# Moving the first batch's early folds from GpSimd to VectorE, and the first weights ahead, in a fused attention, Fourier and MLP kernel

## The chip, the cores and the metric

The kernel runs on one core of a Trainium2 chip. The metric is the time of one execution on the device in microseconds (us), the median over several runs. Smaller is better. The engines are PE (TensorE, matmuls), DVE (VectorE), ACT (ScalarE), POOL (GpSimd) and SP (SyncE, which here only issues DMAs).

## The reference: what is computed

Chunked attention with a few memory keys, whose result goes through a Fourier mix over sequence and features, a normalisation, and a two-layer MLP with a residual:

```
# q, k, v: [4, 8, 768, 64]; mem_k, mem_v: [4, 8, 8, 64]
for each chunk of 32 queries:            # keys: 8 memory + 16 left + 32 own + 8 right
    a = softmax(q_c @ k_full.T / 8);  out_c = a @ v_full
x  = out as [4, 768, 512]
u  = x + real(fft(fft(x, axis=1), axis=2))
un = (u - mean) / sqrt(var + 1e-6)       # over the 512 features
result = u + relu(un @ w_ch1) @ w_ch2    # [512, 2048], [2048, 512]
```

## The kernel before

**Stages.** A batch b has 768 rows and 8 heads, taken as four pairs of heads. Pair n = 4b + i goes through `attention(n)`; after four pairs the batch goes through a Fourier stage (`first_fourier` for b = 0, `fourier(b)` for the others), then `columns_of`, and later `mlp(b)`.

*Attention.* Queries and keys are loaded by GpSimd's DMA queue (`e_load_qk`, L343 and L347, three buffers each), values by SP's (`e_load_v`, four buffers `va`). For batches 0 to 2 PE turns queries and keys by transposes (`turn`, L374: `trq`, `trk`), and ACT or DVE copies them out (`e_qT` L392, `e_kT` L417). For the last batch (TURNED = 3) SP turns them by a DMA transpose (`e_flip_q` L379, `e_flip_k` L383 into `kU`), and DVE copies the keys into place (`e_kT`, L412). For each half g of a pair: scores (`e_scores`, L430, into `sc`, of which there is one PSUM slot), exponentials on ACT (`e_exp`, L438), values (`e_values`, L454, into `xa` or, in the first batch's second halves, `xo`), and the normalisation on DVE (`e_norm`: reciprocal L464, product L465 into `xsb`). Half g holds row tiles 3g to 3g+2 of the batch.

*Fourier stage of the first batch.* The transform over rows and columns uses symmetry: columns are folded first. For each row half g and each parity `par` there is `g_zy` (L594: sum or difference of two column blocks), then for each `ab` a first fold `g_ff(..., last=0)` (L608 to L613: `zy` plus or minus reversed columns of `xsb`; it needs pairs 0 to 2) and a last fold `g_ff(..., last=1)` (L613 with `ff` as input; it needs pair 3 also). ACT casts the result to fp16 (`g_hi`, L629), DVE subtracts to get the rest (`g_lo`, L633, into `lo` or `hl`), and PE multiplies both with sine and cosine tables (`g_rows`, L666, into `ps`). GpSimd does a small extra row (`g_mid`, L639 to L642), which PE multiplies in `g_row` (L653). ACT and DVE evict `ps` (`e_up` L538, `e_rest` L543), then come the columns on PE (`e_columns`, L677, into `pm`), sums and statistics on DVE (L683, L691), the centred rows on ACT (L697).

*Later batches.* `fourier(b)` folds over rows as well; the mirrored half of the rows goes through HBM (`x_rows`, `x_back`, `xr`) and is added on the way back (L584).

*MLP.* PE computes `ph` (`e_ch1`, L739, in groups of 4 matmuls), ACT the relu (L747), PE `pc` (`e_ch2`, L754), DVE the residual (L779). The weights come in eight loads of 512 KB on GpSimd's queue (`w1` L975, `w2` L979), converted to fp16 on the way.

**What sets the order.** Nothing is issued in the order of the source. Every piece of work is a task of the class `Plan`: an engine, an expected cost, the tasks it comes after, the buffers it takes and gives back, and a rank. `Plan.order` plays the tasks against a clock made of these costs and lists them by planned start; they are emitted in that order. On the chip every engine then works through its own list strictly in order, and waits only where data or buffers demand it. Three arguments matter here: `behind=t` holds a task in the planning until task t has been placed; it makes no wait on the chip. `lag=x` makes the planner place a task only when what it comes after is x us old in planned time. A `filler` task (MLP matmuls) and the `idle` matmuls (L830, on zeros, keep PE going in the beginning, until the first `g_lo` is placed) fill PE where nothing else can be placed.

**What the change touches.** In `first_fourier` the early tasks of the first row half (g = 0) are on DVE and those of the second (g = 1) on GpSimd. In `weights` the loads of w1 are placed behind the keys of pair 5. `t_gate` is a tiny GpSimd copy that waits for the values of pair 3, so that loads for batch 1 don't start sooner.

Of the kernel before, what the change touches and what calls it, by code (L numbers as in the profile page):

```python
# [14 lines left out]
ALU = mybir.AluOpType  # L15
# [21 lines left out]
class Plan:  # L37
# [15 lines left out]
    def add(self, engine, cost, emit, after=(), take=(), give=(), rank=None, moved=0.0,  # L53
            loose=False, late=0.0, filler=False, behind=None, lag=0.0, pick=None, grain=0.1, head=1.0):
        t = dict(engine=engine, cost=cost, emit=emit, after=[a for a in after if a is not None],
                 take=take, give=give, rank=len(self.tasks) if rank is None else rank,
                 moved=moved, done=None, at=None, no=len(self.tasks), loose=loose,
                 late=late, filler=filler, behind=behind, lag=lag, pick=pick, grain=grain, head=head)
        self.tasks.append(t)
        return t  # L60
# [117 lines left out]
def kernel(  # L178
# [11 lines left out]
    nc = tc.nc  # L190
# [3 lines left out]
    P = 128  # L194
    NST = S // P
    NDT = DM // P
# [393 lines left out]
    def g_zy(par, g):  # L590
        if g == 0:
            zy_of[0, par] = fpool.tile([P, NST, P], FP32, tag="unT", bufs=2, name="zy0")
        xb, sl, eng = xs[0], slice(3 * g, 3 * g + 3), nc.gpsimd if g == 1 else nc.vector
        eng.tensor_tensor(zy_of[0, par][:, sl], xb[:, sl, 0:P], xb[:, sl, HD:HD + P],  # L594
                                ALU.add if par == 0 else ALU.subtract)

    def g_ff(par, ab, g, last):
        if (ab, g, last) == (0, 0, 0):
            ff_of[0, par] = fpool.tile([P, 2, NST, P], FP32, tag="fold", bufs=2, name="ff0")
        xb, sl = xs[0][:, 3 * g:3 * g + 3], slice(3 * g, 3 * g + 3)  # L600
        zy, ff = zy_of[0, par][:, sl], ff_of[0, par][:, ab, sl]
        eng = nc.gpsimd if g == 1 and not last else nc.vector
        plus = ab == par
        if last:
            plus = plus == (par == 0)
        if not last:
            if ab == 0:
                eng.tensor_copy(ff[:, :, 0], zy[:, :, 0])  # L608
            elif par == 0:
                eng.memset(ff[:, :, 0:1], 0.0)  # L610
        elif (par, ab) == (1, 1):
            eng.tensor_tensor(ff[:, :, 0], xb[:, :, P], xb[:, :, HD + P], ALU.subtract)
        eng.tensor_tensor(ff[:, :, 1:P], (ff if last else zy)[:, :, 1:P],  # L613
                                rev_ap(xb, 2 * P - 1 + HD * last, P - 1, [[DM, 3]]),
                                ALU.add if plus else ALU.subtract)

# [252 lines left out]
    def attention(n):  # L869
        nonlocal t_gate  # L870
        b, pr = seq[n]
        first = b == 0
        lq, lk = [add("POOL", 1.6 if b >= TURNED else 0.9, lambda i=i: e_load_qk(n, i),
                      take=(("qs", "ks")[i],), moved=3.1 if b >= TURNED else 1.2, grain=0.032 if b >= TURNED else 0.1, late=LATE if b else 2.0,
                      behind=t_gate if n == HP else t_xr[b - 2] if n == TURNED * HP else t_ck.get(n - 1),
                      rank={0: -4 + i, 1: -1.2 + 0.1 * i, 2: 10 + 0.1 * i}.get(n)) for i in range(2)]
        lv = add("SP", 2.5, lambda: e_load_v(n), [t_ones[n] if n < NV else None],
                 behind=t_x2.get(b - 2),
                 take=("va",), moved=2.6, grain=0.031, head=0.4, late=(0.0, 4.0, LATE, LATE)[b])
        t_lv[n] = lv  # L880
        t_ck[n] = lk
        if n == HP - 1:
            def e_gate():
                nc.gpsimd.tensor_copy(gate[64:65], va[n % NV][64:65, 1, NT - 1, 0:1])

            t_gate = add("POOL", 0.1, e_gate, [lv])
        mk = t_mk[n] = add("DVE", 0.2, lambda: e_mkT(n), [t_mkT, t_kTz[n % NKT], t_mk.get(n - 1)],
                           take=("kTb",), behind=t_norm.get((HP - 1, 1)) if n in (HP, HP + 1) else None)
        if b >= TURNED:
            eq = add("SP", 1.2, lambda: e_flip_q(n), [lq], take=("qT",), give=("qs",),  # L890
                     late=5.0, loose=True, behind=t_flip[0])
            t_flip[0] = tk = add("SP", 1.2, lambda: e_flip_k(n), [lk, t_uz], take=("kU",),
                                 give=("ks",), late=5.0, loose=True, behind=eq)
            ek = add("DVE", 0.6, lambda: e_kT(n), [tk, mk], give=("kU",))
        else:
            tq = add("PE", 0.40, lambda: e_turn_q(n), [lq, t_idb], take=("tr",), give=("qs",))
            dve = ("DVE", nc.vector.tensor_copy) if n < HP else ("ACT", None)
            eq = add("ACT", 0.80, lambda: e_qT(n), [tq], take=("qT",), give=("tr",),
                     rank=SINES - 0.5 if n == 0 else None)
            ktag = "acc" if first else "tr"  # L900
            tk = add("PE", 0.43, lambda: e_turn_k(n), [lk, t_idb, t_kz if n == 0 else t_kzs],
                     take=(ktag,), give=("ks",))
            ek = add(dve[0], 1.25 if dve[1] else 1.04, lambda: e_kT(n, dve[1]), [tk, mk],
                     give=(ktag,))
        for g in range(2):
            s_ = add("PE", 0.32, lambda g=g: e_scores(n, g), [eq, ek], take=("sc",),
                     give=("qT", "kTb") if g == 1 else ())
            t_sc[n, g] = s_
            t_exp[n, g] = x_ = add("ACT", 1.12, lambda g=g: e_exp(n, g),
                     [s_, t_masks, t_after.get(n)], take=("e1",), give=("sc",))  # L910
            tag = "mlp" if first and g == 1 else "xa"
            v_ = add("PE", 0.85, lambda g=g: e_values(n, g), [x_, lv, t_low[n % NV]], take=(tag,),
                     rank=len(plan.tasks) + (50 if (n, g) == (2, 1) else 25) if first else None,
                     give=("e1", "va") if g == 1 else ("e1",))
            take = ("xsb",) if g == 0 and n % HP == 0 else ()
            t_norm[n, g] = add("DVE", 0.78, lambda g=g: e_norm(n, g),
                               [v_, t_norm[n - n % HP, 0] if (n % HP, g) != (0, 0) else None],
                               take=take,
                               give=(tag,))
        return x_  # L920
# [47 lines left out]


    w2v = moe_w_ch2.rearrange("(ht p) m -> p ht m", p=P)  # L970
    t_w1, t_w2 = [], []

    def weights(n):
        if n == HP + 1:
            t_w1.extend(add("POOL", 0.7, lambda dt=dt: nc.gpsimd.dma_start(  # L975
                w1_sb[:, dt, :], moe_w_ch1[ts(dt, P), :]), moved=2.4, grain=0.32, late=2.0,
                behind=t_ck[n], rank=t_ck[n]["rank"] + 0.1) for dt in range(NDT))
        else:
            t_w2.extend(add("POOL", 0.7, lambda g=g: nc.gpsimd.dma_start(  # L979
                w2_sb[:, ts(g, 4), :], w2v[:, ts(g, 4), :]), moved=2.6, late=2.0,  # L980
                behind=t_ck[n], rank=t_ck[n]["rank"] + 0.1) for g in range(4))

    def first_fourier():
        t_rest, t_mid, t_row, pre = {}, {}, {}, {}
        for g in range(2):
            for par in range(2):
                early = ("DVE", "POOL")[g]
                zy = add(early, (0.5, 1.1)[g], lambda par=par, g=g: g_zy(par, g),
                         [t_norm[0, g], t_norm[1, g], t_sines],
                         take=("unT",) if g == 0 else (), rank=20.1 if g else None)  # L990
                for ab in range(2):
                    pre[par, ab, g] = add(early, (0.62 if ab == 0 else 0.5) + 0.8 * g,
                                          lambda par=par, ab=ab, g=g: g_ff(par, ab, g, 0),
                                          [zy, t_norm[2, g]], rank=20.2 + 0.1 * par if g else None,
                                          take=("fold",) if (ab, g) == (0, 0) else (),
                                          give=("unT",) if (ab, g) == (1, 1) else ())
            t_mid[g] = add("POOL", 0.9, lambda g=g: g_mid(g), [t_norm[2, g], t_norm[3, g]],
# [3 lines left out]
            for par in range(2):  # L1001
                for ab in range(2):
                    end = (ab, g) == (1, 1)
                    ff = add("DVE", 0.5 + 0.1 * par * ab,
                             lambda par=par, ab=ab, g=g: g_ff(par, ab, g, 1),
                             [pre[par, ab, g], t_norm[3, g]])
                    hi = add("ACT", 0.5, lambda par=par, ab=ab, g=g: g_hi(par, ab, g), [ff],
                             take=(("hl",), ("hT",))[par] if (ab, g) == (0, 0) else ())
                    lo = add("DVE", 0.48, lambda par=par, ab=ab, g=g: g_lo(par, ab, g), [hi],
# [206 lines left out]
```

The softmax here doesn't subtract the row's maximum and nothing guards it: scores larger than these inputs give would overflow.

## Time and profile before

The time is 289.14 us (median of 3 runs, 289.12 to 289.34). The profiled execution has a span of 287.7 us, at a PE clock of 1.00 throughout.

| engine | busy us | share of the span |
|---|---|---|
| PE | 272.2 | 95% |
| DVE | 169.5 | 59% |
| ACT | 159.9 | 56% |
| POOL | 65.7 | 23% |

The busy share of an engine is an average over stages that differ, so it has to be read by stage. Of PE's time, 8.2 us are the 35 `idle` matmuls, all before 34 us. The largest groups of work on PE are `ph` (88.5 us), `pc` (84.2 us, both with modelled ends), and `xa` (26.4 us). DMA moves 39.92 MB, at a mean of 139 GB/s, and at about 200 GB/s between 44 and 80 us.

A line of a timeline reads: start (us), duration (us), engine, line, operation, output <- inputs, shapes, count, and in brackets the idle time of the engine before it and what ended it. If several instructions are merged (x2), the duration is that of the whole stretch.

### The profile page before, as it was taken

Reading aid. Unit: us, or ns where it says so; the run is one execution under the profiler, and the core shown is the slowest. Engines: PE = TensorE matmul, PEld = TensorE weight load, DVE = VectorE, ACT = ScalarE, POOL = GpSimd, SP = SyncE. Lnnn points to the kernel's source line nnn. Section 1 sums busy time; section 2 is a strip of 40 time slices with the busy share of each in tenths; the row PEclk is TensorE's granted clock in tenths of the full one; section 3 lists DMA queues with packets and bytes.
Section 4 is the critical chain, followed back from the end, with each engine's and each line's share of the span. In section 5 each row is a group of like instructions: output and inputs, shape, how many; then the busy total and the mean of one; then the engine's idle time right before and its main releaser. Section 6 shows DMA issues by size and latency. Waiting matters only on the chain.

```text
span 287.7 us, 7165 instructions
## 1 busy us (share of the span) xinstructions
PE 272.2 (95%) x2947; PEld 172.2 (60%) x2947; DVE 169.5 (59%) x350; ACT 159.9 (56%) x286; POOL 65.7 (23%) x115
## 2 busy tenths in 40 slices
PE   0599889999999999999999999999999999999995
PEld 0476578865565777556766556566654644645644
DVE  7968999862159967958874984985672012012012
ACT  6887345788766676835764485517660721722710
POOL 8844794341210182261001020010020000000000
PEclk9999999999999999999999999999999999999999
DMA  6999999999998999999993756766142504003204
GB/s 108 198 184 162 180 154 204 203 201 196 207 189 219 171 199 153 164 112 238 173 209 86 166 113 108 175 107 195 21 85 84 106 0 117 32 34 100 51 36 109
DMA packets 116112, 39.92 MB, mean 139 GB/s; under 512 B 104560, under 2 KB 111472, under 8 KB 116080
## 3 DMA queue, kind: packets, MB, share of 16 engines
q1 hardware_dynamic: 93888, 23.54, 46.4%
q0 software_dynamic: 21472, 15.21, 32.9%
q10 hardware_dynamic: 720, 0.72, 0.8%
q8 instruction: 23, 0.38, 0.6%
q14 instruction: 9, 0.07, 0.1%
HBM read 37.36 MB, written 13.37 MB: 176 GB/s over the span
## 4 chain that ended last, share of the span: by engine, by line
PE 83%; DMA 6%; DVE 5%; POOL 4%; issue 1%; POOLq 0%
PE pc L754 28%; PE ph L739 26%; PE xa L454 7%; DMA qs<-in_q_dram 6%; PE ps L526 5%; PE pm L677 4%; PE sc L430 3%; DVE ff L613 2%; PE ps L666 2%; PE trk L374 2%; PE trq L374 1%; PE pc L760 1%; PE idle L830 1%; DVE hl L633 1%; DVE xsb L465 1%
## 5 line engine op out<-in xcount | busy, mean ns | idle before, releaser
L747 ACT ACTIVATE hT<-ph 128x384 f16<-128x384 f32 x128 | 62.0, 491 | 50.8 <-PE ph L739 49.9
L739 PE MATMUL ph<-unT,w_sb 128*128 128x384 f16 x512 | 88.5, 326 | 0.0
L754 PE MATMUL pc<-w_sb,hT 128*128 128x512 f16 x368 | 84.2, 380 | 0.0
L739 PEld LDWEIGHTS <-w_sb 128*128 128x128 f16 x512 | 48.4, 98 | 31.7 <-issue 0.6
L754 PEld LDWEIGHTS <-hT 128*128 128x128 f16 x368 | 34.5, 98 | 39.1 <-issue 0.2
L779 DVE SCALAR_TENSOR_TENSOR osb<-pc,rstd,xsb 128x512 f32<-128x512 f32 x23 | 17.2, 750 | 63.8 <-PE pc L754 61.6
L438 ACT ACTIVATE e<-sc,mbias 128x384 f32<-128x384 f32 x64 | 33.6, 577 | 22.7 <-PE sc L430 22.6
L454 PEld LDWEIGHTS xa<-va,e 128*64 128x64 f32 x672 | 22.5, 141 | 7.0 <-issue 5.6
L454 PE MATMUL xa<-va,e 128*64 128x65 f32 x672 | 26.4, 229 | 0.0
L697 ACT ACTIVATE un<-xsb,mu_s 128x512 f16<-128x512 f32 x24 | 17.2, 719 | 7.7 <-DVE mu_s L692 7.7
L538 ACT CAST up<-ps 128x386 f16<-128x386 f32 x16 | 9.6, 602 | 19.6 <-PE ps L526 17.4
L691 DVE BATCH_NORM_STATS2 st<-xsb 128x6 f32<-128x512 f32 x24 | 16.6, 692 | 0.8
L465 DVE TENSOR_TENSOR xsb<-xa,zs 128x384 f32<-128x384 f32 x28 | 15.6, 558 | 1.0
L464 DVE RECIPROCAL zs<-xa 128x6 f32<-128x6 f32 x28 | 5.3, 189 | 17.6 <-PE xa L454 17.6
L543 DVE TENSOR_TENSOR up<-ps,up 128x386 f16<-128x386 f32 x16 | 9.6, 598 | 9.2 <-ACT up L538 9.1
L683 DVE TENSOR_TENSOR xsb<-pm,xsb 128x512 f32<-128x512 f32 x15 | 10.0, 673 | 5.0 <-PE pm L677 5.0
L569 POOL DMA_DIRECT2D xr<-x_back x3 | 2.3, 780 | 46.6 <-DMA x_back<-x_rows 46.6
L430 PEld LDWEIGHTS <-kTb 64*128 64x128 bf16 x384 | 7.7, 97 | 8.7 <-issue 6.8
L430 PE MATMUL sc<-qT,kTb 64*128 64x64 bf16 x384 | 11.6, 196 | 0.9 <-POOL va L315 0.9
L516 DVE TENSOR_TENSOR lo<-ff,hi 128x768 f16<-128x768 f32 x12 | 11.4, 954 | 1.5 <-ACT hi L511 1.3
L486 DVE TENSOR_TENSOR zy<-xsb 128x768 f32<-128x768 f32 x12 | 11.4, 955 | 0.2
L503 DVE TENSOR_TENSOR ff<-pq 128x762 f32<-128x762 f32 x12 | 11.3, 947 | 0.0
(153 smaller groups left out, 355.1 us busy)
## 6 DMA issues: line engine op xcount, KB each, us to landing
va<-in_v_dram SPq DMA_DIRECT2D x32, 220.0 KB
w_sb<-in_moe_w_ch_dram POOLq DMA_DIRECT2D x8, 512.0 KB, 14.7
out_dram<-osb SPq DMA_DIRECT2D x12, 256.0 KB
qs<-in_q_dram POOLq DMA_DIRECT2D x12, 192.0 KB, 6.8
ks<-in_k_dram POOLq DMA_DIRECT2D x12, 192.0 KB, 6.7
x_rows<-xsb POOLq DMA_DIRECT2D x3, 768.0 KB, 5.5
xr<-x_back POOLq DMA_DIRECT2D x3, 768.0 KB, 5.4
out_rows<-osb SPq DMA_DIRECT2D x9, 256.0 KB
```

The lines of the kernel that those rows point to most:

```text
L430: nc.tensor.matmul(sc[:, hh, t6, :], kT[r0:r0 + 64, t, :], qT[r0:r0 + 64, ts(t, 64)], start=True, stop=True, tile_position=(r0, 0))
L438: nc.scalar.activation(e1[:, :, :, ts(half, 32)], sc[:, :, 0:6, ts(half, 32)], AFT.Exp, bias=mbias[:, half:half + 1], scale=1.0 / math.sqr ...
L454: nc.tensor.matmul(xa[64 * half:64 * half + 64, st, hh, 0:65], e1[:, hh, t6, :], v1[:, hh, 6 * g + t6, 0:65], start=True, stop=True)
L465: nc.vector.tensor_tensor(xs[b][:, 3 * g:3 * g + 3, 2 * pr * D:(2 * pr + 2) * D] .rearrange("p s (h d) -> p s h d", h=2), xa[:, :, :, 0:D] ...
L526: nc.tensor.matmul(out_[:, sp, :], part[:, ab, sp * 3 + st, c0:c1], tab[:, sp, st, :], start=(st == 0 and i == 0), stop=(st == 2 and i == 1))
L677: nc.tensor.matmul(pm[:, par, :], lhs, rhs[:, par, :], start=(im == 0), stop=(im == 3))
L691: nc.vector.bn_stats(st6, xs[b][:, kt, :])
L697: nc.scalar.activation(un, xs[b][:, kt, :], AFT.Identity, bias=mu_of[b][:, kt, 0:1], scale=-1.0)
L739: nc.tensor.matmul(ph[:, 0:384], w1_sb[:, dt, ts(ht, P)], unT_of[b][:, dt, sh * 384:(sh + 1) * 384], start=(dt == 0), stop=(dt == NDT - 1))
L747: nc.scalar.activation(hT_of[b, sh][:, ht, :], ph[:, 0:384], AFT.Relu, bias=0.0, scale=-1.0)
L754: nc.tensor.matmul(pc_of[b, sh, stl], hT_of[b, sh][:, ht, ts(stl, P)], w2_sb[:, ht, :], start=(ht == 0), stop=(ht == NHT - 1))
L779: nc.vector.scalar_tensor_tensor(osb, pc, rstd_of[b][:, st:st + 1], xs[b][:, st, :], ALU.mult, ALU.add)
```

## The change

The change has three parts.

1. The early folds of the second row half (g = 1), which are two `g_zy` and four `g_ff(..., last=0)` with their small copies and a memset, go from GpSimd to DVE. On GpSimd only `g_mid` remains of this stage. Their planned costs and ranks become those of the first half.
2. The loads of w1 are no longer placed behind the keys of pair 5, but behind the task `t_mark`, the first last-fold of the second row half (par 0, ab 0) on DVE; what follows the keys of pair 5 is now placed behind the last load of w1 (`t_ck[n] = t_w1[-1]`). It is meant to put the weights where GpSimd is done with this stage.
3. The copy of DMA-turned keys (`e_kT` of the last batch) gets `lag=4.0`: it is placed at least 4 us after the planned landing of the transpose, so that DVE should not stand in front of a transpose that is late.

```diff
     def g_zy(par, g):
         ...
-        xb, sl, eng = xs[0], slice(3 * g, 3 * g + 3), nc.gpsimd if g == 1 else nc.vector
-        eng.tensor_tensor(zy_of[0, par][:, sl], xb[:, sl, 0:P], xb[:, sl, HD:HD + P],
+        xb, sl = xs[0], slice(3 * g, 3 * g + 3)
+        nc.vector.tensor_tensor(zy_of[0, par][:, sl], xb[:, sl, 0:P], xb[:, sl, HD:HD + P],
                                 ALU.add if par == 0 else ALU.subtract)

     def g_ff(par, ab, g, last):
         ...
-        eng = nc.gpsimd if g == 1 and not last else nc.vector
         ...
-        eng.tensor_tensor(ff[:, :, 1:P], (ff if last else zy)[:, :, 1:P],
+        nc.vector.tensor_tensor(ff[:, :, 1:P], (ff if last else zy)[:, :, 1:P],
                                 rev_ap(xb, 2 * P - 1 + HD * last, P - 1, [[DM, 3]]),
                                 ALU.add if plus else ALU.subtract)
         ...
-            ek = add("DVE", 0.6, lambda: e_kT(n), [tk, mk], give=("kU",))
+            ek = add("DVE", 0.6, lambda: e_kT(n), [tk, mk], give=("kU",), lag=4.0)
         ...
-    t_w1, t_w2 = [], []
+    t_w1, t_w2, t_mark = [], [], []

     def weights(n):
         if n == HP + 1:
             t_w1.extend(add("POOL", 0.7, lambda dt=dt: nc.gpsimd.dma_start(
                 w1_sb[:, dt, :], moe_w_ch1[ts(dt, P), :]), moved=2.4, grain=0.32, late=2.0,
-                behind=t_ck[n], rank=t_ck[n]["rank"] + 0.1) for dt in range(NDT))
+                behind=t_mark[0], rank=t_ck[n]["rank"] + 0.1) for dt in range(NDT))
+            t_ck[n] = t_w1[-1]
         ...
-                early = ("DVE", "POOL")[g]
-                zy = add(early, (0.5, 1.1)[g], lambda par=par, g=g: g_zy(par, g),
+                zy = add("DVE", 0.5, lambda par=par, g=g: g_zy(par, g),
                          [t_norm[0, g], t_norm[1, g], t_sines],
-                         take=("unT",) if g == 0 else (), rank=20.1 if g else None)
+                         take=("unT",) if g == 0 else ())
                 for ab in range(2):
-                    pre[par, ab, g] = add(early, (0.62 if ab == 0 else 0.5) + 0.8 * g,
+                    pre[par, ab, g] = add("DVE", (0.62 if ab == 0 else 0.5),
                                           lambda par=par, ab=ab, g=g: g_ff(par, ab, g, 0),
-                                          [zy, t_norm[2, g]], rank=20.2 + 0.1 * par if g else None,
+                                          [zy, t_norm[2, g]],
         ...
+                    if (par, ab, g) == (0, 0, 1):
+                        t_mark.append(ff)
```

Beside the named instructions the change moves others, since the planner works the whole order out anew. Read from the instruction lists as built: PE has 28 `idle` matmuls instead of 35; a key turn and both scores of pair 4 stand ahead of the first batch's columns, where one key turn did; from pair 6 on attention and MLP matmuls are interleaved in another way; and in the last batch the scores of pairs 12 to 15 stand further back.

More of the change, by code (lines that the diff above doesn't have):

```diff
@@ L607, in g_ff @@
             if ab == 0:
-                eng.tensor_copy(ff[:, :, 0], zy[:, :, 0])
+                nc.vector.tensor_copy(ff[:, :, 0], zy[:, :, 0])
             elif par == 0:
-                eng.memset(ff[:, :, 0:1], 0.0)
+                nc.vector.memset(ff[:, :, 0:1], 0.0)
         elif (par, ab) == (1, 1):
-            eng.tensor_tensor(ff[:, :, 0], xb[:, :, P], xb[:, :, HD + P], ALU.subtract)
-        eng.tensor_tensor(ff[:, :, 1:P], (ff if last else zy)[:, :, 1:P],
+            nc.vector.tensor_tensor(ff[:, :, 0], xb[:, :, P], xb[:, :, HD + P], ALU.subtract)
+        nc.vector.tensor_tensor(ff[:, :, 1:P], (ff if last else zy)[:, :, 1:P],
                                 rev_ap(xb, 2 * P - 1 + HD * last, P - 1, [[DM, 3]]),
```

## The prediction

> **What bounds the kernel now.** I read the slices of the page first, then busy time by stage, then the timelines of VectorE (DVE), GpSimd (POOL) and TensorE (PE) between 22 and 56 us, then the chain of waits. The slices of PE, VectorE and GpSimd (7.2 us each):
>
> ```profile
> PE   0599889999999999999999999999999999999995
> DVE  7968999862159967958874984985672012012012
> POOL 8844794341210182261001020010020000000000
> ```
>
> PE is full from slice 7 to the end; before that it isn't. Busy time by stage (columns PE, PEld, DVE, ACT, POOL, then clock, DMA share, GB/s) says where the free time lies:
>
> ```profile
> 30.00:37.00 7.00, 5.68 (x76) 3.95 (x75) 6.90 (x15) 1.99 (x5) 5.07 (x12) 1.00 1.21 178
> 37.00:44.00 7.00, 6.17 (x70) 5.38 (x68) 7.00 (x14) 3.07 (x7) 7.00 (x10) 1.00 0.90 159
> 44.00:50.00 6.00, 5.97 (x82) 5.03 (x80) 5.49 (x13) 3.42 (x6) 2.39 (x4) 1.00 1.04 203
> 50.00:56.00 6.00, 6.00 (x106) 4.76 (x105) 5.68 (x13) 4.94 (x9) 1.39 (x2) 1.00 1.11 205
> ```
>
> From 47 to 284 us PE waits for nothing (every later stage reads 10.00 of 10.00, and no PE wait is listed after 45 us). So the end is the time at which PE is filled, plus a fixed amount of matmuls, plus a tail of 3 us. Only what PE wastes before 47 us can be gained. Between 30 and 44 us VectorE is the full engine: it folds the first batch. Its timeline there:
>
> ```profile
> 27.59 1.81 DVE L613 TENSOR_TENSOR ff<-zy,xsb 128x381 f32<-128x381 f32 x2
> 30.08 2.95 DVE L613 TENSOR_TENSOR ff<-zy,xsb 128x381 f32<-128x381 f32 x2
> 33.77 1.02 DVE L613 TENSOR_TENSOR ff<-ff,xsb 128x381 f32<-128x381 f32 x2
> 34.93 0.56 DVE L465 TENSOR_TENSOR xsb<-xo,zs 128x384 f32<-128x384 f32 x1
> 37.81 2.61 DVE L633 TENSOR_TENSOR hl<-ff,hl 128x384 f16<-128x384 f32 x2
> 42.76 1.01 DVE L633 TENSOR_TENSOR hl<-ff,hl 128x384 f16<-128x384 f32 x2
> ```
>
> and GpSimd's:
>
> ```profile
> 26.65 2.34 POOL L594 TENSOR_TENSOR zy<-xsb 128x384 f32<-128x384 f32 x2
> 31.64 0.98 POOL L613 TENSOR_TENSOR ff<-zy,xsb 128x381 f32<-128x381 f32 x1
> 37.44 2.58 POOL L613 TENSOR_TENSOR ff<-zy,xsb 128x381 f32<-128x381 f32 x2
> 39.96 0.68 POOL L347 DMA_DIRECT2D ks<-in_k_dram  x1
> 40.63 2.20 POOL L975 DMA_DIRECT2D w_sb<-in_moe_w_ch_dram  x4
> ```
>
> The same VectorE fold takes 1.02 us for two when GpSimd rests, and 1.81 to 2.95 when GpSimd runs a fold at the same time; the subtraction of L633 goes from 1.01 to 2.61. GpSimd's help is paid for on the engine it helps. One more pair, from the chain of waits:
>
> ```profile
> 53.66 17.74 DMA qs<-in_q_dram
> 71.44 0.53 PE trq L374 x16
> ```
>
> The queries of pair 7, issued behind all weights, land as PE comes to turn them, with about 0.1 us to spare. This is no loss now, but it is the next wall.
>
> **What the skill says.** "SBUF — State Buffer", section "Who interferes with whom": a VectorE instruction with two SBUF inputs takes its second one through a read interface that GpSimd shares, and the pair is locked for a whole instruction. Trace: agrees; folds and subtractions (two SBUF inputs) stretch, the normalisation L465 (one input in PSUM) stays at 0.56. "DMA: Bandwidth & Descriptors", section "Issuing engines are not separate DMA queues": all DMAs run on the same 16 engines and interleave. Trace: agrees, the mean DMA share is 0.9 to 1.2 from 22 to 80 us, so starting the weights sooner brings little new bandwidth.
>
> **Part 1: early folds to VectorE.** Spacing of starts is the price: 0.47 us a fold (36.88 to 37.81 for two), 0.48 for zy, 0.1 for the small copy, 0.05 for the memset. Added: 2 x 0.48 + 4 x 0.47 + 0.25 = 3.1 us. Removed, by form: the four ff<-zy mean 1.23 against 0.547 free (2.7 us), the four hl 0.945 against 0.547 (1.6), two small copies 0.48 against 0.16 (0.6): 4.9 us. Net 1.8 us less, and the new zy also use 0.6 us of idle before 26.20.
>
> Walked in the built order, with PE and ScalarE as in the trace: kTb copy from 24.34 to 25.5; two zy 26.5; normalisation (0.7) and fold 27.75; wait for the values (PE done 27.97), normalisation 28.8; two folds 29.9; normalisation 30.7; two folds 31.6; last normalisation 32.3 (now 35.4). Then 0.94 + 1.41 + 0.54 + 1.1 + 0.47 + 1.04 + 1.41: the second half's first subtraction can start at 39.2, those of its first three parts end at 39.7, 40.2, 40.65, and, after a fold, two kTb copies and one eviction, the last at 42.5.
>
> PE: the four first-half groups of 12 rows matmuls (1.02 us each) run from 35.5, after mid rows and a key turn that now stand in front of them, to 39.6; the second half 39.8 to 43.85, bound by VectorE at its start, then by PE. Next in PE's order come the scores of pair 4, a query turn (0.46), the second scores. There is one PSUM slot for scores, and ScalarE does two evictions (until 44.6) and the exponentials (1.0) before it is free: PE stands from 44.6 to 45.65 (new wait). Columns start at 45.95, now 47.23.
>
> Gain, counted as waste. From 31.36 (end of the last values) to the columns: now 15.87 us, of which useful 0.47 query turn + 0.3 + 2.4 mid rows + 8.12 rows (96 x 0.0845) + 0.47 key turn = 11.8, wasted 4.1 (nine fill matmuls 1.5, GpSimd's mid 1.3, VectorE 0.9, rest 0.4). Then: 14.6 us, with 1.02 more useful work in it (two scores, one query turn), wasted 1.8. **Gain 2.3 us.** PE is full from there, so it reaches the end one for one. Fifth and sixth columns need sums that VectorE gives at about 52.5: 0.3 us lost. PE's order has four fewer changes of kind (0.1 us each, as ph x4 takes 0.76 at a change and 0.65 inside a run): 0.3 to 0.4 won. Sum 2.3 us.
>
> **Part 2: weights behind the first fold.** The mark orders the planner only; no wait is added. In the built order the four loads stand right behind the mid operations, about 33.9 instead of 40.63, and the keys of pair 5 stand before everything (about 28 instead of 39.96). Queued behind are the queries of pair 6, w2, those of pair 7. PE first needs w1 at about 55.4; the slowest w1 landing was 13.3 us, so 49.5: nothing on the path. Pair 7's queries: PE asks for them at 71.44 - 2.3 - 0.65 = 68.5 (built order: two scores and one values more, three ph groups fewer ahead). The chain of loads starts 6.7 us sooner and without 192 KB of keys (1 us) in front, but shares the engines with one and a half v loads more (0.85 MB at 180 GB/s, 4.2 us, minus half a v load, 1.4): landing at about 66.5, bounds 64 (no sharing) and 70.5 (full engines give no gain but that of the missing keys). I take 66.5: cost nothing, hidden by ph.
>
> **Part 3: copies of turned keys later.** A planning delay of 4 us for four VectorE copies of 0.43 us. No VectorE wait for these transposes is in the trace, so nothing is removed. In the built order the last batch's values end some 20 matmuls (3 us) later; MLP matmuls stand in their place. Behind them are folds (PE has 8.6 us of work against a VectorE chain of 6.5) and mirrored rows, which landed at 196.8 for a first use at 206.9. Cost nothing.
>
> **The rivals.**
> (a) The stretch isn't GpSimd's doing: folds stay at 1.23 us, VectorE gets 3.1 us more, minus 0.6 of idle. PE fills 2.5 us later, minus 1.0 for work moved ahead: 290.6, slower. Against it: the same form at 0.547 as soon as GpSimd rests. Chance 0.06. With it go stalls later on that I can't see, as the copies in part 3 (290): 0.04.
> (b) Transfers are the next wall: pair 7 lands at 69 to 70.5, PE stands 0.5 to 2 us: 288.1. For it: DMA share near 1. Chance 0.2.
> (c) What I gain is lost again at score slot, bank and VectorE waits: within 0.2%. Chance 0.06.
> (d) The score wait doesn't come up, as ScalarE is earlier: 1 us more, 285.8. Chance 0.08.
>
> **The numbers.** Likeliest, at 0.56: 289.14 - 2.3 = 286.8 us. Range 285.5 to 288.8, which takes in most of (b) and (d) and leaves out (a) and part of (c). Faster by over 0.2% (under 288.56): 0.56 + 0.08 + 0.2 = 0.84; within 0.2% 0.06; slower 0.10.
>
> **What would show it.** Right: ff<-zy and hl at 0.55 us; last L465 of the first batch near 32.3; 28 fill matmuls for 35; w1 issued near 34; columns from about 46 with the scores of pair 4 before them; PE without a gap after 47. Wrong: folds still over 1 us; a PE gap in front of pair 7's query turn near 68 us, released by its DMA; VectorE waiting for a transposed key; a gap in front of the last batch's rows or MLP.

## The result and the profile after

The changed kernel takes **286.27 us** (median of 5 executions, 286.13 to 286.98) against 289.34 before (5 executions beside it, 289.12 to 290.34): a ratio of 0.9897, 95% interval 0.9874 to 0.9919. Run a second time, among the last experiments, it took 286.74 (286.09 to 287.19) against 289.13 before: 0.9915, 0.9898 to 0.9932. The prediction was 286.8, in a range of 285.5 to 288.8. Ratios are taken over executions within 1.5% of a kernel's fastest; some of the kernels below stand still in some executions and not in others, so I compare medians of all their executions.

The slices of the page for TensorE (PE) and GpSimd (POOL), 7.1 us each:

```profile
PE   0599998999999999999999999999999999999995
POOL 8844643131210183170001020101002000000000
```

Counted from 0, PE's slices 4 and 5 (29 to 43 us) were 8 and are 9, slice 6 has become 8, and GpSimd's 7 and 9 in slices 4 and 5 are 6 and 4. Busy time by stage, with the columns of the prediction (length, PE, PEld, DVE, ACT, POOL, clock, DMA share, GB/s):

```profile
30.00:37.00 7.00, 6.70 (x108) 5.56 (x107) 6.64 (x19) 2.54 (x5) 5.82 (x13) 1.00 1.20 208
37.00:44.00 7.00, 6.77 (x90) 6.34 (x89) 6.61 (x18) 4.65 (x9) 2.61 (x4) 1.00 1.08 212
44.00:50.00 6.00, 5.15 (x86) 4.45 (x85) 4.91 (x12) 3.68 (x8) 1.92 (x3) 1.00 1.14 197
50.00:56.00 6.00, 5.76 (x115) 4.55 (x112) 5.86 (x14) 4.13 (x7) 1.26 (x2) 1.00 1.23 197
```

PE was busy 11.85 us of the 14 from 30 to 44, and is now busy 13.47. In the next two stages it is idle for 0.85 and 0.24 us. The timeline of VectorE has the operations that were stretched before:

```profile
31.35 0.56 DVE L465 TENSOR_TENSOR xsb<-xo,zs 128x384 f32<-128x384 f32 x1
36.66 1.02 DVE L612 TENSOR_TENSOR ff<-zy,xsb 128x381 f32<-128x381 f32 x2
41.87 0.55 DVE L632 TENSOR_TENSOR hl<-ff,hl 128x384 f16<-128x384 f32 x1
```

Folds and subtractions are at 0.55 us (1.02 for two); none is longer. The last normalisation ends at 31.9 (35.5 before), the last subtraction at 42.4. On GpSimd's timeline nothing but the middle sums stands ahead of the weights, which go out at 33.10 instead of 40.63:

```profile
33.10 2.20 POOL L974 DMA_DIRECT2D w_sb<-in_moe_w_ch_dram  x4
```

And PE's timeline, with its only gaps after 45 us, and the query turn of pair 7, which before started 0.04 us after its data had landed (71.40 and 71.44):

```profile
45.32 0.35 PE L430 MATMUL sc<-qT,kTb 64*128 64x64 bf16 x12 [0.85 <-ACT e L438]
52.36 0.39 PE L676 MATMUL pm<-cosD,dn 128*128 128x256 f16 x2 [0.24 <-DVE xsb L682]
67.79 0.51 PE L374 MATMUL trq<-ident_b,qs 96*64 96x96 bf16 x16
```

The score slot's wait is there, as forecast (0.85 us), so is the fifth column's (0.24), and the query turn waits for nothing. The columns start at 45.60 (47.23 before).

One caution on that pair of traces. Twelve score matmuls take 0.50 us in the beginning and 0.35 later; the short durations set in at 17.9 us in the profiled run of after and at 19.1 in that of before, with the same order of work. (0.50 is also what they take at a granted clock of 0.50, in a timeline shown below; in the beginning the profile lists a granted clock of 1.00.) That moves the first batch's last value matmuls by 0.5 us and is not the change's doing: in the second profile of after they come 0.2 us later than before, and its columns at 45.85. So the two traces give the change 2.7 and 3.0 us.

A useful way to split every run below is at the first column matmul: what comes before it is the first batch's stage, and **the rest**, from there to the end of the span, is a fixed amount of work plus whatever PE waits for. The time is the median of a kernel, the other columns are of its one profiled execution, and they can differ: before, part 2 alone and part 3 alone have medians within 0.3 us of each other and columns at 47.23, 46.24 and 47.66. So I take a start of the columns to be good to about 0.7 us either way.

| kernel | time, us | columns start | rest | PE waits in the rest (0.2 us and more) |
|---|---|---|---|---|
| before | 289.34 | 47.23 | 240.5 | none |
| after | 286.27 | 45.60 | 239.0 | 0.24 |
| after, again | 286.74 | 45.85 | 239.0 | 0.23 |
| part 1 alone | 291.77 | 46.29 | 243.4 | values 2.43, turned keys 0.38 |
| part 2 alone | 289.42 | 46.24 | 240.4 | none (an execution of 288.30) |
| part 3 alone | 289.62 | 47.66 | 240.6 | 0.27 |
| parts 1 and 2 | 286.60 | 46.08 | 238.8 | 0.2 |
| before, GpSimd writes only | 287.09 | 45.06 | 240.3 | none |
| after, spare GpSimd folds | 290.48 | 49.80 | 239.0 | 0.3 |
| after, weights early | 290.54 | 46.35 | 239.2 | 0.24 (an execution of 287.23) |
| part 1, weights late | 293.28 | 46.13 | 245.3 | turned keys 3.99, queries 0.69 |
| parts 1 and 3 | 289.00 | 47.49 | 240.7 | values 1.70 |
| parts 1 and 3, weights late | 288.01 | 45.83 | 239.6 | 0.37 (an execution of 287.15) |
| after, scores later | 288.10 | 44.51 | 241.8 | sums of the second batch 1.57, 0.24 |

### The profile page after: what moved, and what is told of

It reads as the page before. It is cut to its first block, busy times and chain, and to the rows that moved or that the text cites. A ratio compares the mean times of both kernels' runs of the same rounds, so it can differ in the third digit from the quotient of the medians.

```text
span 284.6 us, 7154 instructions
## 1 busy us (share of the span) xinstructions
PE 269.5 (95%) x2940; PEld 171.6 (60%) x2940; DVE 166.2 (58%) x359; ACT 158.2 (56%) x286; POOL 57.5 (20%) x106
## 4 chain that ended last, share of the span: by engine, by line
PE 81%; DMA 7%; DVE 6%; SPq 2%; ACT 2%; issue 1%; POOL 0%; DVEq 0%; POOLq 0%
PE ph L738 30%; PE pc L753 29%; PE xa L454 7%; PE ps L526 5%; DMA va<-in_v_dram 4%; PE pm L676 4%; PE sc L430 2%; DMA qs<-in_q_dram 2%; DVE ff L612 1%; PE trq L374 1%; SPq L356 1%; PE trk L374 1%; DMA out_dram<-osb 1%; DVE xsb L682 1%; PE pm L577 1%
## 5 line engine op out<-in xcount | busy, mean ns | idle before, releaser
L738 PEld LDWEIGHTS <-w_sb 128*128 128x128 f16 x512 | 48.6, 98 | 32.3 <-issue 0.8
L690 DVE BATCH_NORM_STATS2 st<-xsb 128x6 f32<-128x512 f32 x24 | 16.6, 692 | 0.7
L511 ACT CAST hi<-ff 128x768 f16<-128x768 f32 x12 | 10.0, 831 | 4.3 <-DVE ff L503 4.3
```

What stands on the lines that cost most here:

```text
L690: nc.vector.bn_stats(st6, xs[b][:, kt, :])
L738: nc.tensor.matmul(ph[:, 0:384], w1_sb[:, dt, ts(ht, P)], unT_of[b][:, dt, sh * 384:(sh + 1) * 384], start=(dt == 0), stop=(dt == NDT - 1))
```

## The experiments

### The parts one by one

The theory was that part 1 carries the whole gain. Each part of the diff shown above was put on the kernel before by itself, and parts 1 and 2 together.

**Part 1 alone** (the folds on VectorE; w1 still behind `t_ck[n]`, no lag).

> Part 1 alone: early folds on VectorE, w1 placed behind the keys of pair 5 as before, no delay for the turned keys. In its order w1 is issued right behind those keys, about 28 us, ahead of the mid operations. Theory A (the gain is the end of the stretch of VectorE folds, carried one for one to PE): VectorE folds at 0.55 us, 286.3 to 287.0, so at least 2.3 of the 3 us. Rival B (the gain is that of the weights being placed better): 288.5 or more. Rival C (the planning delay of the copies is needed, without it VectorE stands before a transpose): 288 or more with a VectorE wait for kU.

Measured: 291.77 us (22 executions, 289.31 to 296.38), ratio 1.006 (1.0037 to 1.0084). That is slower than before. Yet the folds do what they should: they take 0.55 us, and the columns start at 46.29. All of the loss is in the rest, which is 4.6 us longer than with parts 1 and 2. Its PE waits:

```profile
PE xa L454 <- DMA va<-in_mem_v_dram: 2.4, 1, 2.4
PE sc L430 <- DVE kTb L412: 0.4, 1, 0.4
```

The first is new: values of pair 6, at 68.1 to 70.53 us. Around it, busy time by stage:

```profile
68.00:72.00 4.00, 1.57 (x33) 1.50 (x31) 0.08 (x1) 0.65 (x2) 0.00 (x0) 0.79 0.96 183
72.00:76.00 4.00, 4.00 (x75) 2.64 (x71) 1.19 (x4) 2.24 (x4) 0.63 (x1) 0.78 0.94 158
```

The third column from the right is PE's clock: 0.79 and 0.78. After the gap it was granted at half for about 3.4 us (in slices of 1 us it reads 0.66, 0.50, 0.50, 0.63), so 1.7 us more are lost. With 2.43 and 0.38 that makes 4.5 us, against the 4.6 that the rest is longer (parts 1 and 2 wait 0.24 us there, which this run does not).

Why are the values late? SyncE's own timeline, which issues them, in part 1 alone:

```profile
29.47 14.32 SPq L356 DMA_DIRECT2D va<-in_v_dram  x2
60.51 0.32 SPq L365 DMA_DIRECT2D va<-in_mem_v_dram  x1
```

and in the whole change:

```profile
30.83 3.94 SPq L356 DMA_DIRECT2D va<-in_v_dram  x2
51.31 0.31 SPq L365 DMA_DIRECT2D va<-in_mem_v_dram  x1
```

In part 1 alone the keys of pair 5 no longer wait behind GpSimd's folds, and w1, placed behind them, goes out at 28.78. The issue of a pair of value loads that starts right after it stands for 14.32 us, and the last piece of pair 6 is issued at 60.51 and arrives at 70.39 (9.88 us in the chain of waits), while PE wants it at 67.8. In the whole change it is issued at 51.31 for a use at 67.04. In the kernel before it was issued at 36.94 for a use at 76.50.

**Part 2 alone** (`behind=t_mark[0]` on the kernel before) and **part 3 alone** (`lag=4.0`).

> Part 2 alone: folds of the second half stay on GpSimd. The instruction order is nearly that of the kernel before, because the mark falls where GpSimd is busy with folds. Theory A: 289.1 to 289.4, no change. Rival B: 287.5 or less.

> Part 3 alone: the copies of turned keys placed 4 us later in the plan. No VectorE wait for these transposes is in the trace of before, so theory A: 289.0 to 289.6, no change beyond a few changes of kind on PE (0.1 us each; two pieces more in PE's order). Rival C: 288.5 or less.

Measured: 289.42 us (ratio 0.9994, 0.9977 to 1.001) and 289.62 (1.0007, 0.9989 to 1.0025). Neither moves the time. In part 2 alone w1 goes out at 39.64 instead of 40.63: GpSimd's folds still stand ahead of it, so the new place changes hardly anything.

**Parts 1 and 2** (the whole change without the lag).

> Parts 1 and 2, without part 3. Theory A: as the whole change, 286.0 to 286.6, and no VectorE wait for kU over 0.3 us. Rival C: 287 or more, with VectorE waiting for a transposed key and PE behind it.

Measured: 286.60 us (six executions, 285.91 to 290.70; ratio 0.9901, 0.9874 to 0.9929), as the whole change. So part 2, worth nothing alone, is needed beside part 1, and part 3 moves the median by nothing that can be measured. Two of the six executions stand apart, at 288.06 and 290.70, where none of the eleven of the whole change is above 287.19; six are too few to say whether the lag keeps such executions away.

### Is it GpSimd's reading that stretches VectorE?

**Before, with GpSimd writing only.** The six early folds of row half 2 become memsets, with every other engine's list as before. They are zeros then, and this half's part of the Fourier rows is left out:

```diff
+        if g == 1:
+            nc.gpsimd.memset(zy_of[0, par][:, sl], 0.0)
+            return
         ...
+        if g == 1 and not last:
+            nc.gpsimd.memset(ff, 0.0)
+            return
```

> The kernel before, with the six early folds of row half 2 on GpSimd replaced by GpSimd memsets of the same tiles, so that the even and odd folds of that half are zeros and its part of the first batch's Fourier rows is left out; TensorE, VectorE and ScalarE keep the order of before. Theory A (GpSimd's folds stretch VectorE's work on the same row half, and that holds the rows): the VectorE folds and low parts of row half 1 and 2 between 31 and 42 us fall from 1.0 to 1.5 us each to about 0.55 us, the columns start some 2 to 3 us earlier, and the time is 286.5 to 287.7 us. Rival (VectorE's work in that stretch is slow for another reason, or the rows are held by something else): the VectorE operations stay at 1.0 us and over, and the time stays at 289 to 290 us.

Measured: 287.09 us, ratio 0.9922 (0.9908 to 0.9937). GpSimd's timeline and VectorE's beside it:

```profile
28.77 0.79 POOL L607 MEMSET ff<- 128x384 f32 x2
34.48 0.77 POOL L607 MEMSET ff<- 128x384 f32 x2
```

```profile
29.43 1.01 DVE L619 TENSOR_TENSOR ff<-zy,xsb 128x381 f32<-128x381 f32 x2
34.48 1.01 DVE L619 TENSOR_TENSOR ff<-ff,xsb 128x381 f32<-128x381 f32 x2
35.41 1.01 DVE L639 TENSOR_TENSOR hl<-ff,hl 128x384 f16<-128x384 f32 x2
```

VectorE's folds and subtractions are at 0.55 us (1.01 for two), in the old order, even while GpSimd writes at that very moment. The columns start at 45.06, 2.2 us sooner, and the rest is that of before (240.3): a gain of 2.4 us with no new order at all. A rival would be that GpSimd, with less to do, is merely quicker with the middle sums, for which PE waited 1.29 us in before. But there GpSimd had itself waited 1.19 us for VectorE's normalisation before it could start them, so that wait too goes back to VectorE.

**After, with spare folds on GpSimd.** Their results go into a tile that nothing reads; the lists of the other engines are those of after.

```diff
+        if g == 1:
+            nc.gpsimd.tensor_tensor(spare, xb[:, sl, 0:P], xb[:, sl, HD:HD + P], ALU.add)
         ...
+        if g == 1 and not last:
+            nc.gpsimd.tensor_tensor(spare[:, :, 1:P], zy[:, :, 1:P],
+                                    rev_ap(xb, 2 * P - 1, P - 1, [[DM, 3]]), ALU.add)
```

> The kernel after, in which GpSimd repeats the six early folds of row half 2 into a spare tile that nothing reads; the order of TensorE, VectorE, ScalarE and SyncE is that of after, and the first weights are issued behind the spare folds, some 4 to 5 us later. Theory A (work of GpSimd on the rows stretches VectorE's): VectorE's folds of 0.55 us go back to 1.0 us and over while GpSimd folds, the columns start 1.5 to 2.5 us later than in after, and the time is 288 to 289.5 us. Rival (what helped was another order of the work, not the missing GpSimd folds): VectorE's folds stay at 0.55 us and the time is 286 to 287 us.

Measured: 290.48 us (289.86 to 291.75), ratio 1.0044 (1.0028 to 1.006). GpSimd and VectorE:

```profile
35.70 5.23 POOL L619 TENSOR_TENSOR spare<-zy,xsb 128x381 f32<-128x381 f32 x4
```

```profile
37.02 1.80 DVE L615 TENSOR_TENSOR ff<-zy,xsb 128x381 f32<-128x381 f32 x2
38.74 1.34 DVE L638 TENSOR_TENSOR hl<-ff,hl 128x384 f16<-128x384 f32 x1
40.01 0.95 DVE L610 COPY ff<-zy 128x3 f32<-128x3 f32 x1
```

The same operations, 1.02 for two and 0.55 in after, are stretched again, and even a copy of three columns goes from 0.16 to 0.95. The columns start at 49.80. The rest is 239.0, that of after: the 4.2 us that the first stage loses reach the end one for one. 0.6 of them arise in the first 14 us, before any spare fold runs. The loss is well over the 1.5 to 2.5 us I expected, and VectorE's list accounts for it: its first subtraction of the second row half starts at 43.20, against 38.99 in after, and 3.2 us of this delay arise between a small copy at 36.15 (35.11 in after) and that subtraction, beside the four spare folds. PE's wait of 1.70 us for ScalarE's half of a fold belongs to it, since ScalarE had waited for VectorE's fold. PE's waits for late middle sums (0.32 and 0.23) and for a query (0.71) come before these and add nothing, as PE then waits for VectorE all the same. The rival, that only the order helped, is out in both directions.

### What part 2 is for: the weights and the values

**After, with the weights early.** The four loads of w1 are issued inside the load of the keys of pair 5; the planner still counts them at their old place, so every other engine's list is that of after.

```diff
+        if (n, i) == W1_AT:                      # (HP + 1, 1)
+            for dt in range(NDT):
+                nc.gpsimd.dma_start(w1_sb[:, dt, :], moe_w_ch1[ts(dt, P), :])
         ...
-            t_w1.extend(add("POOL", 0.7, lambda dt=dt: nc.gpsimd.dma_start(
-                w1_sb[:, dt, :], moe_w_ch1[ts(dt, P), :]), moved=2.4, ...
+            t_w1.extend(add("POOL", 0.7, lambda dt=dt: None, moved=2.4, ...
```

> The kernel after with one thing moved: GpSimd issues the four first weight loads right behind the key load of pair 5 (about 28 us, as in part 1 alone) and not behind the middle sums (33.1 us). The order of TensorE, VectorE, ScalarE and SyncE is that of after. Theory V (in part 1 alone the early weights hold up the value loads: one SyncE issue of value rows was blocked for 14.3 us from 29.5 us on, and TensorE waited 2.4 us for values at 68 to 70.5 us and then ran some 4 us at a lower granted clock): the same long issue, a TensorE wait for values of 1 to 3 us near 67 to 71 us, and 289 to 291.5 us. Rival O (part 1 alone was slow by the order that the planner wrote for it, or by the copy of turned keys that waited for its transfer): no wait for values, and 286 to 287.2 us.

Measured: 290.54 us (ratio to before 0.9979, 0.9944 to 1.0014), about 4 more than after, but in two heaps: five executions at 286.9 to 288.9 and nine at 290.3 to 293.6, with nothing between. The profiled one is of the first heap (287.23). It has a long issue on SyncE, though not directly behind w1 (29.99 to 32.18):

```profile
35.32 11.84 SPq L361 DMA_DIRECT2D va<-in_v_dram  x2
```

The last piece of pair 6 is issued at 55.3, for a use at 67.8: 12.5 us of room, where after has 15.7 and part 1 alone 7.3. Its values came in time. A landing of about 10 us, as in part 1 alone, leaves it 2 us to spare. That the second heap is made of executions in which this room did not suffice is what theory V says and what the distance of some 4 us between the heaps fits. The mean granted clock of each execution speaks for a gap on PE in them: it is 0.988 to 0.994 in all nine and 0.999 to 1.000 in the five, and 0.994 over 288 us is 1.7 us lost, as after the gap in part 1 alone. (Of the 117 executions of before that ran beside these kernels, nine have 0.994 or less, so the clock alone is no proof.) No trace of the second heap was taken, so which wait it was stays inferred. What is shown is that the place of w1 alone costs about 4 us in the median; by the ratio it is some 2 us, and the interval is still clear of both of after (0.9874 to 0.9919 and 0.9898 to 0.9932).

**Part 1 with the weights late.** Part 1 alone, w1 issued with the keys of pair 6 (`W1_AT = (HP + 2, 1)`), all other lists as in part 1 alone.

> Part 1 alone with one thing moved: GpSimd issues the four first weight loads behind the middle sums and the key load of pair 6 (about 33 to 34 us) and not behind the key load of pair 5 (28.8 us). The order of TensorE, VectorE, ScalarE and SyncE is that of part 1 alone, and the copy of turned keys has no lag. Theory V (the early weights hold up the value loads): no TensorE wait for values, no drop of the granted clock near 70 us, and 286.3 to 287.6 us. Rival O (the order that the planner wrote for part 1 alone is what is slow): 290 to 292 us with the weights late too. Rival L (the lag is what was missing): the copy of turned keys still waits near 128 us and TensorE waits behind it by more than the 0.4 us of part 1 alone, 288 us and over.

Measured: 293.28 us (22 executions; 21 of them at 292.47 to 295.37, one at 288.27). The ratio (1.005, 0.9997 to 1.0103) rests on three executions and settles nothing; by all of them it is worse still. With w1 alone moved, SyncE issues the last piece of pair 6 at 42.84 instead of 60.51, and the wait for values is gone:

```profile
42.84 0.31 SPq L370 DMA_DIRECT2D va<-in_mem_v_dram  x1
```

So far theory V is right, but the time is not what it said. PE's timeline around a new gap:

```profile
123.72 1.04 PE L758 MATMUL pc<-w_sb,hT 128*128 128x512 f16 x4
128.74 0.50 PE L435 MATMUL sc<-qT,kTb 64*128 64x64 bf16 x12 [3.99 <-DVE kTb L417]
129.18 3.25 PE L758 MATMUL pc<-w_sb,hT 128*128 128x512 f16 x8
132.36 0.35 PE L435 MATMUL sc<-qT,kTb 64*128 64x64 bf16 x12
```

VectorE's side of it:

```profile
128.25 0.43 DVE L417 COPY kTb<-kU 128x1056 bf16<-128x1056 bf16 x1 [5.39 <-DMA kU<-ks]
```

The copy of pair 12's turned keys stands on VectorE in front of a transpose that was issued at 120.62 and is not there until 128.25; a copy of memory keys and a normalisation are queued behind it, and PE's scores wait for it 3.99 us. Then PE runs at half clock again (0.50 granted from 129 to 131 us): eight matmuls of L758 take 3.25 us (1.90 elsewhere). 3.99, 1.5 for the clock and 0.69 for a query make 6.2 us, against the 6.5 by which its rest exceeds that of parts 1 and 2. The mean granted clock is 0.986 to 0.994 in those 21 executions and 1.000 in the one at 288.27. In part 1 alone the transpose landed at the same time (128.03), but PE, held up by 4 us at 70 us, came later and lost only 0.38 us to it. One stall hid the other. So theory V was half of the truth, and rival L, that the lag is missing, the other half.

### What part 3 is for: the copies of turned keys

**Parts 1 and 3**, w1 early as in part 1 alone; and the same **with w1 late**, all other lists equal.

> Parts 1 and 3 without part 2: VectorE folds and the lag of the turned keys' copy, the first weights issued at about 28 us as in part 1 alone. Theory W (part 1 alone loses by two waits: values of pair 6 that arrive late behind the early weights, and the copy of turned keys that stands before its transfer has landed): the lag takes the second wait away and leaves the first, so a TensorE wait for values of 1 to 3 us near 68 to 71 us, none for the copy of turned keys, 289 to 291 us. Rival K (only the copy of turned keys costs; values never): 286 to 287.2 us. Rival O (the lag is of no account): a wait for turned keys near 123 to 128 us, and 290.5 to 293 us.

> The run before this one in the list (parts 1 and 3) with the first weight loads moved behind the middle sums and the key load of pair 6 (about 34 us); TensorE, VectorE, ScalarE and SyncE keep its order. Against the earlier run of part 1 with late weights (293.28 us, TensorE waiting 4.0 us for the copy of turned keys) it adds the lag alone. Theory W (both waits are then gone): no TensorE wait of over 1 us after 50 us, and 286 to 287.2 us. Rival O (the lag is of no account, the order behind part 1 is slow by itself): 289 us and over.

Measured: 289.00 us (ratio 0.9985, 0.9965 to 1.0005) and 288.01 (0.9965, 0.9948 to 0.9983). In the first, PE's timeline has one gap after 50 us:

```profile
71.00 0.80 PE L454 MATMUL xa<-va,e 128*64 128x65 f32 x20 [1.70 <-DMA va<-in_mem_v_dram]
```

Its first two copies of turned keys stand at 143.57 without a wait. In the second there is neither that gap nor one for turned keys; PE waits once, 0.4 us. The lag, put on part 1 with late weights, makes the planner write another order from the last batch's scores on, and takes 5.3 us off (293.28 to 288.01). The late weights take 1.0 off parts 1 and 3, with intervals that overlap, so that this step is not clear of the noise. In the traces each of the two waits is removed by its own part, as theory W said. But 288.01 is 1.3 us more than the whole change beside it, and above the 286 to 287.2 that I expected. Its profiled execution (287.15) shows no wait that would account for it; the room between issue and use of the values is as small as 4.8 us in it (pair 8, issued by 75.8, used at 80.67), which may fail in other executions. That stays open.

### A try to go further

**After, with the second scores of pair 4 planned behind the second column task**, so that PE does not stand in front of the score slot for 0.85 us:

```diff
             s_ = add("PE", 0.32, lambda g=g: e_scores(n, g), [eq, ek], take=("sc",),
+                     behind=t_cols.get(1) if (n, g) == (HP, 1) else None,
```

> The kernel after, with the second scores of pair 4 planned behind the second column task, so that they do not stand on TensorE before the one score slot is free (the wait of 0.85 us at 45.3 us). The planner writes another order behind that. Theory S (that wait is still on the path): 285.3 to 285.9 us, and the wait is gone. Rival (the planner gives it back in changes of kind or in another wait): 286.1 us and over.

> The kernel after, unchanged, beside the three others. Theory W (in the whole change both waits have room: values of pair 6 are issued 22 us before their use, and the copy of turned keys stands 4 us and more behind its landing): 286 to 287 us, with none of its executions at 290 us and over. Rival (the whole change only shifts the same danger, and some of its executions pay it): some executions at 289 to 292 us.

Measured: 288.10 us (287.34 to 289.14) beside 286.74 for after. The wait is gone and the columns start at 44.51, 1.1 us sooner than in after. But the planner wrote the rest anew, and there PE stands once more:

```profile
163.22 0.39 PE L676 MATMUL pm<-cosD,up 128*128 128x256 f16 x2 [1.57 <-DVE xsb L586]
```

VectorE had waited 2.9 us for the mirrored rows of a later batch (`xr`, which come back through memory), and PE for VectorE. The rest is 241.8, 2.8 us longer: the new wait is 1.57 of it, the second scores, which now stand behind the start of the columns, about 0.3, and the remaining 0.9 is not accounted for. The rival was right: more is given back at 163 us and elsewhere than is won at 45. None of the eleven executions of after was above 287.2, so nothing speaks for either wait being paid in some executions of the whole change. (Its values of pair 6 are issued 15.7 and 16.6 us before their use in the two traces, not 22 as the expectation has it.) No version here is shown to be faster.

## Why the prediction was right, and where it was not

**What bounds the kernel** (PE is full after the columns, so the end is their start plus a fixed amount): right for the change. The spare folds show it best, with a loss of 4.2 us at the columns and a rest of 239.0 with and without them. The amount is fixed only as long as no new wait comes up behind the columns, as in part 1 alone (243.4).

**Part 1, the stretch**: right. Removing GpSimd's reads alone gives 2.4 us, putting them back costs 3.7 to 4.2. The Trainium skill, "SBUF — State Buffer", section "Who interferes with whom", says that a VectorE instruction with two inputs in SBUF contends with a GpSimd instruction that reads SBUF, not with one that only writes it. Both halves are seen here: two folds in 1.01 us beside GpSimd's memsets, in 1.80 and more beside its folds. The small copy has one input in SBUF, so the sentence does not cover it; that it is held as well (0.95 us instead of 0.16) is only observed. Rival (a), that folds stay slow on VectorE, is out.

**Part 1, the walk**: the last normalisation was put at 32.3 and came at 31.9, the last subtraction at 42.5 and 42.4. The score slot's wait was put at 1.05 us and measured 0.85; rival (d), without it, is out. The columns were put at 45.95 and came at 45.60 and 45.85, or 46.1 and 45.7 counted from the same start as before. Fill matmuls: 28, as listed.

**The sum**: 2.3 us were forecast, less than came; medians of two comparisons give 3.1 and 2.4, traces 2.7 and 3.0 once the start is set aside. The term that was too small lies behind the columns: I had 1.02 us of work moved ahead, 0.3 to 0.4 for fewer changes of kind and 0.3 lost at the fifth column, in all 1.0 to 1.1, and the rest became 1.5 shorter. The fifth column did cost 0.24. About 0.4 us of the gain in the rest is not accounted for by my terms.

**Part 2, "cost nothing"**: the figure was right and the working incomplete. I followed what w1's earlier issue does to the queries of pair 7: landing put at 66.5, with bounds 64 and 70.5. They were issued at 45.38, and even the longest landing of a query load in that trace, 19.6 us, would have them there by 65.0, for a use at 67.79. (I read 0.1 us to spare for them in before; the trace has PE idle for 0.05 us just there, so they had none.) Rival (b) named transfers as the next wall, and I looked for it at those queries. The wall was nearer at the value loads, which I counted only as traffic: their lead for pair 6 fell from 39.6 us to 15.7, and in part 1's own order it would have been 7.3, less than the 10 us that a landing takes there. So part 2 is not free of effect; it is what keeps part 1's gain, and as far as the values go, the right figure was luck. I costed each part against the kernel before, where its effect is nothing, and not against the other parts.

**Part 3, "cost nothing"**: right for the median of the whole change, which parts 1 and 2 reach without it. "No VectorE wait for these transposes is in the trace, so nothing is removed" held for before, but an order in which the copy comes sooner has that wait: 5.39 us on VectorE, and 5.3 us in the time. The four copies in the whole change stand without a wait at 135.83, 139.75, 152.79 and 168.60. The transpose of pair 12 took 7.4 and 7.6 us from issue to release in the two runs that waited for it, and at most 4.6 in before and 4.5 with parts 1 and 2, where the copy found it landed. Why, no run here tells. With 7.6 us the copy in parts 1 and 2 would have waited too, so the lag may be worth more than the medians show; that is not tested.

**Rival (c)**, that the gain is lost again, did not come true for the change, but did for part 1 alone and for the later scores, by other waits than those I named.

## What to carry to other kernels

Work given to GpSimd beside a VectorE that is full can cost VectorE more than it takes off it, when both read the on-chip memory (SBUF): compare the same form's duration with and without the helper before sharing work out. And before an engine's load is lightened, list what is queued behind it on that engine: here it was a weight load, whose earlier issue held up another queue's loads, 40 us ahead of where it hurt. A part of a change that does nothing alone may still be what keeps another part's gain, so test it with that part and not only by itself.

## What the runs showed of the hardware that I had not expected

- A gap on PE can cost more than its length. After gaps of 2.43 and 3.99 us PE's granted clock was 0.50 for about 3 us (1.7 and 1.5 us lost); after gaps of 1.57 and 1.70 us it stayed at 1.00. The Trainium skill, "TensorE: Matmul & The Clock Gate", section "Part 1: The HAM clock gate (the "warmup" mystery)", puts the loss of clock at an idle window of about 3.4 us; here 2.43 us were enough.
- A DMA issue itself can stand: one pair of value loads held SyncE for 14.32 us when four weight loads of 512 KB had just been issued from GpSimd (13.57 in parts 1 and 3, 11.84 in after with the weights early), and what is behind it in SyncE's list waits too. The same pair takes 0.80 us at 25.90 in after. What holds it, no run here shows.
- The same kernel, in the same order, can fall into two heaps of times: with w1 early, nine of fourteen executions lie at 290.3 us and over and the other five at 288.9 and under, which is taken here for a transfer that is late in some executions and not in others. A profile without a wait does not speak for the other executions.
